# Two engines for the first Q and K copies, masks sooner on VectorE, and two memsets ahead of the first V loads

## The chip, the cores, the metric

One core of a Trainium2 chip. The metric is the device time of one execution in microseconds (us), as a median of runs. A profile's "span" runs from the first to the last instruction of one profiled execution and is some 2 us shorter than the time of that execution.

## The reference

```python
def reference(q, k, v, moe_w_gate, moe_w_val, moe_w_out):   # cut and joined
    scores = q @ k.T / sqrt(64), masked to abs(i - j) <= 32     # 8 batches, 8 heads, 576 x 64
    attn = softmax(scores) @ v
    x = attn with the heads side by side                        # 4608 x 512
    g, val = x @ w_gate, x @ w_val                              # 512 x 1536
    return (g * sigmoid(g) * val) @ w_out                       # 4608 x 512, float32
```

## The kernel before

It works through eight batches: sliding-window attention of a batch, then the feed-forward part on its rows, on TensorE most of the time. The change touches the opening alone: the attention of batch 0, before TensorE has feed-forward work to fill its gaps. Its helpers (cut):

```python
    def cast_qk(st, cast):
        t16 = qk16.tile([128, J9, 2, D], FP16, tag="qk16", name="t16")
        cast(t16.rearrange("p j h d -> p h j d"),
             st.rearrange("p h (j d) -> p h j d", d=D))
        return t16
    def transpose_qk(t16, pool=None):
        ps = (pool or ps_c).tile([128, 2048], FP16, tag="a" if pool is ps_a else "c",
                                 name="qk_ps")
        for j in range(J9):
            nc.tensor.transpose(out=ps[:, 128 * j:128 * j + 128], in_=t16[:, j, :, :],
                                identity=ident)
        return ps[:, 0:J9 * 128].rearrange("c (j a p) -> c a p j", j=J9, a=2)
    def place_k(src, b, half, cast):
        cast(kT[b][:, 2 * half:2 * half + 2, 32:32 + S].rearrange(
            "c a (p j) -> c a p j", j=J9), src)
# place_q: the same into qT, without the offset of 32
# quad_scores(ms, F): 16 score matmuls into a ps_a tile (2 buffers), then two exps on ScalarE
# quad_mask(ms, F): one multiplication by the mask on VectorE
# shift_v(b, m, cast): two copies that build the V tiles which straddle two loads
# pair_av(m): 16 matmuls attention times V, then the normalization on VectorE
# turn_x: transposes of the result, copied to xT by ScalarE
# idle_mms(n): n filler matmuls of 512 columns on TensorE, whose result nobody reads
```

The opening, from the first loads to the first feed-forward unit:

```python
    st = [load_qk2(src, 0, half) for half in range(2) for src in (q, k)]
    nc.gpsimd.memset(v16[1][:, :, :, 64:66], 1.0)
    load_v(0, range(5))
    for s in range(len(SLABS)):
        load_w_slab(moe_w_gate, wg16, s)
        load_w_slab(moe_w_val, wv16, s)
        if s == 1:
            shift_v(0, 0, cast_pool)
    for s in range(4):
        load_wo(s)
    nc.gpsimd.memset(v16[1][0:32, 0, :, :], 0.0)
    nc.gpsimd.memset(v16[1][96:128, NT - 1, :, :], 0.0)
    c16 = [cast_qk(t, cast_dve) for t in st]
    idle_mms(6)
    place_q(transpose_qk(c16[0], ps_a), 0, 0, cast_act)
    idle_mms(2)
    place_k(transpose_qk(c16[1]), 0, 0, cast_act)
    idle_mms(4)
    place_q(transpose_qk(c16[2], ps_a), 0, 1, cast_act)
    quad_scores((0, 1), 0)
    idle_mms(1)
    place_k(transpose_qk(c16[3]), 0, 1, cast_dve)
    quad_scores((2, 3), 0)
    idle_mms(3)
    quad_mask((0, 1), 0)
    quad_scores((0, 1), 1)
    quad_mask((2, 3), 0)
    shift_v(0, 1, cast_dve)
    quad_mask((0, 1), 1)
    idle_mms(2)
    quad_scores((2, 3), 1)
    shift_v(0, 2, cast_act)
    shift_v(0, 3, cast_act)
    quad_mask((2, 3), 1)
    idle_mms(4)
    pair_av(0)
    pair_av(1, ps_a)
    idle_mms(4)
    pair_av(2, ps_a)
    pair_av(3)

    nxt = [qkst.tile([128, 2, J9 * D], FP32, tag="qkst", name="qk_st") for _ in range(4)]
    for t in nxt:
        nc.vector.memset(t[:, 0, 0:1], 0.0)
    st = [load_qk2(src, 1, half, nxt[2 * half + i]) for half in range(2)
          for i, src in enumerate((q, k))]
    for m in range(4):
        turn_x([m], ps_o, cast_act)
    c16 = [cast_qk(t, cast_pool) for t in st]
    load_v(1, range(5))
    for u in range(FKS):
        ffn1_unit(0, u)
        ...
```

The four loads of Q and K bring the first half of Q, the first of K, the second of Q and the second of K; they are called slices here. PSUM is the memory of the tiles that TensorE's matmuls write in these traces (qk_ps, s_ps, o_ps, xt_ps, gv_ps). Loads from SyncE (load_qk2) move float32 as it is. Loads from GpSimd (V, the weights wg, wv, wo) cast to 16 bits on the way, and GpSimd issues them one after the other, in program order. The weights come in five slabs of columns; unit u of the feed-forward part needs slab 0 for u = 0, slab 1 for u = 1 and 2, slab 2 from u = 3, slab 3 from u = 6, slab 4 from u = 9.

Of the kernel before, what the change touches and what calls it, by code (L numbers as in the profile page):

```python
# [132 lines left out]
def kernel(  # L133
# [10 lines left out]
    nc = tc.nc  # L144

    B, H, S, D = q.shape
# [4 lines left out]
    NT = S // 64  # L151
# [5 lines left out]
    J9 = S // 64  # L157
# [13 lines left out]
    ps_a = fast.enter_context(tc.tile_pool(name="ps_a", bufs=2, space=bass.MemoryType.PSUM))  # L171
# [5 lines left out]
    kT = [const.tile([128, HP, S + 64], FP16, name=f"kT{i}") for i in range(2)]  # L177
    qT = [const.tile([128, HP, S], FP16, name=f"qT{i}") for i in range(2)]
    v16 = [const.tile([128, NT, H, 66], FP16, name=f"v16{i}") for i in range(2)]
# [32 lines left out]
    def load_qk2(src, b, half, st=None):  # L212
        if st is None:
            st = qkst.tile([128, 2, J9 * D], FP32, tag="qkst", name="qk_st")
        nc.sync.dma_start(out=st, in_=src[b, 4 * half:4 * half + 4].rearrange(
            "(f h) (p j) d -> (h p) f (j d)", h=2, j=J9))
        return st
# [15 lines left out]
    def load_v(b, ms):  # L233

        src, dst = v[b].rearrange("h s d -> s h d"), v16[b % 2]
        for m in ms:
            if m == 0:
                nc.gpsimd.dma_start(out=dst[32:128, 0, :, 0:D], in_=src[0:96])
            elif m == 4:
                nc.gpsimd.dma_start(out=dst[0:96, 8, :, 0:D], in_=src[480:576])  # L240
            else:
                nc.gpsimd.dma_start(out=dst[:, 2 * m, :, 0:D],
                                    in_=src[128 * m - 32:128 * m + 96])

    def shift_v(b, m, cast):

        vb, t = v16[b % 2], 2 * m + 1
        cast(vb[0:64, t, :, 0:D], vb[64:128, t - 1, :, 0:D])
        cast(vb[64:128, t, :, 0:D], vb[0:64, t + 1, :, 0:D])
# [12 lines left out]
    def load_wo(s):  # L262
        nc.gpsimd.dma_start(
            out=wo16[:, 3 * s:3 * (s + 1), :],
            in_=moe_w_out.rearrange("(f p) c -> p f c", p=128)[:, 3 * s:3 * (s + 1), :])
# [11 lines left out]
# [14 lines that stand above are left out]
    def place_q(src, b, half, cast):  # L291
        cast(qT[b][:, 2 * half:2 * half + 2].rearrange("c a (p j) -> c a p j", j=J9), src)
# [4 lines that stand above are left out]
# [10 lines left out]
    def score_mms(s, c, m, i, g):  # L307

        b, t = divmod(2 * m + i, NT)
        for e in range(2):  # L310
            half = slice(64 * e, 64 * e + 64)
            nc.tensor.matmul(out=s[:, e, c, :],  # L312
                             lhsT=kT[b % 2][half, g, 64 * t:64 * t + 128],
                             rhs=qT[b % 2][half, g, 64 * t:64 * t + 64],
                             start=True, stop=True)

    def exp_act(o, s):
        nc.scalar.activation(out=o, in_=s, func=AF.Exp, bias=0.0, scale=1.0 / float(D) ** 0.5)  # L318
# [19 lines left out]
    def quad_scores(ms, F):  # L338

        if ms not in quads:  # L340
            quads[ms] = ppool.tile([128, 2, 2, 2, HP, 64], FP16, tag="p2", name="p2_t", bufs=2)
            for n, m in enumerate(ms):
                pts[m] = quads[ms][:, n]
        s = ps_a.tile([128, 2, 8, 64], FP32, tag="a", name="s_ps")
        for n, m in enumerate(ms):
            for i in range(2):
                for f in range(2):
                    score_mms(s, 4 * n + 2 * i + f, m, i, 2 * F + f)
        four = slice(128 * F, 128 * F + 128)
        pv = quads[ms].rearrange("p n e i g q -> p e n i (g q)")  # L350
        for e in range(2):
            exp_act(pv[:, e, :, :, four],
                    s[:, e].rearrange("p (n i f) q -> p n i (f q)", n=2, i=2))

    def quad_mask(ms, F):
        four = slice(128 * F, 128 * F + 128)
        pm = quads[ms].rearrange("p n e i g q -> p (n e i) (g q)")[:, :, four]
        nc.vector.tensor_tensor(out=pm, in0=pm, in1=mask.rearrange("p (a f) q -> p a (f q)", f=2),  # L358
                                op=ALU.mult)
# [3 lines left out]
    def pair_av(m, pool=None, normed=True):  # L363
        p = pts.pop(m)
        if pool is ps_o:
            o = [ps_o.tile([128, 264], FP32, tag="o", name="o_ps") for _ in range(2)]
        else:
            t2 = (pool or ps_c).tile([128, 2, 512], FP32, tag="a" if pool is ps_a else "c",
                                     name="o_ps")
            o = [t2[:, 0, 0:264], t2[:, 1, 0:264]]  # L370
        for h in range(H):
            for i in range(2):
                b, t = divmod(2 * m + i, NT)
                nc.tensor.matmul(  # L374
                    out=o[h // 4][64 * i:64 * i + 64, 66 * (h % 4):66 * (h % 4) + 66],
                    lhsT=p[:, place(b, h)[0], i, place(b, h)[1], :],
                    rhs=v16[b % 2][:, t, h, :],
                    start=True, stop=True)
        if pool is ps_o:
            av_ps[m] = [(o[a].rearrange("p (a h e) -> p a h e", a=1, e=66), slice(a, a + 1))  # L380
                        for a in range(2)]
        else:
            av_ps[m] = [(t2[:, :, 0:264].rearrange("p a (h e) -> p a h e", e=66), slice(0, 2))]
        if normed:
            pair_norm(m)
# [291 lines left out]
    def idle_mms(n):  # L677
        ob = ps_o.tile([128, 512], FP32, tag="o", name="warm")
        mf = mask.rearrange("p a q -> p (a q)")
        for _ in range(n):  # L680
            nc.tensor.matmul(out=ob, lhsT=mf[:, 0:128], rhs=mf[:, 0:512], start=True, stop=True)
# [34 lines left out]

    st = [load_qk2(src, 0, half) for half in range(2) for src in (q, k)]
    nc.gpsimd.memset(v16[1][:, :, :, 64:66], 1.0)
    load_v(0, range(5))
    for s in range(len(SLABS)):  # L720
        load_w_slab(moe_w_gate, wg16, s)
# [2 lines left out]
            shift_v(0, 0, cast_pool)  # L724
    for s in range(4):
        load_wo(s)
    nc.gpsimd.memset(v16[1][0:32, 0, :, :], 0.0)
    nc.gpsimd.memset(v16[1][96:128, NT - 1, :, :], 0.0)
    c16 = [cast_qk(t, cast_dve) for t in st]
    idle_mms(6)  # L730
    place_q(transpose_qk(c16[0], ps_a), 0, 0, cast_act)
    idle_mms(2)
    place_k(transpose_qk(c16[1]), 0, 0, cast_act)
    idle_mms(4)
    place_q(transpose_qk(c16[2], ps_a), 0, 1, cast_act)
    quad_scores((0, 1), 0)
    idle_mms(1)
    place_k(transpose_qk(c16[3]), 0, 1, cast_dve)
    quad_scores((2, 3), 0)
    idle_mms(3)  # L740
    quad_mask((0, 1), 0)
    quad_scores((0, 1), 1)
    quad_mask((2, 3), 0)
    shift_v(0, 1, cast_dve)
    quad_mask((0, 1), 1)
    idle_mms(2)
    quad_scores((2, 3), 1)
    shift_v(0, 2, cast_act)
    shift_v(0, 3, cast_act)
    quad_mask((2, 3), 1)  # L750
    idle_mms(4)
    pair_av(0)
    pair_av(1, ps_a)
    idle_mms(4)
    pair_av(2, ps_a)
    pair_av(3)

# [1 line left out]
# [7 lines that stand above are left out]
# [227 lines left out]
```

## Time and profile before

| kernel before | |
|---|---|
| time, first three runs | 320.48 us median, 319.91 to 320.63 |
| span of the profiled execution | 317.8 us, mean granted TensorE clock 0.993 |
| TensorE busy | 303.6 us, 96% |
| first feed-forward matmul (gv_ps, L427) | 21.84 us |
| fourth slice of Q and K landed | 10.6 us |
| wv's slab 3 landed (issued 17.05) | 30.8 us |

A line of a timeline gives start, duration, engine, source line, operation, what it writes and reads, the count, and in brackets how long the engine sat idle before it and what ended that. In the page's strip of 40 slices a digit is tenths; PEclk is the clock granted to TensorE. The other lines of before stand in the prediction. Two more are needed later, the first feed-forward matmul and the strip of the clock:

```profile
21.84 1.02 PE L427 MATMUL gv_ps<-xT,wg 128*128 128x512 f16 x4 [0.69 <-ACT xT L268]
```

```profile
PEclk9999999999999999999999999999999999999997
```

### The profile page before, as it was taken

The page shows a single profiled execution, that of the slowest core. Times are in us where ns is not written, and L with a number is a line of the kernel's source. Part 1 is how long each engine was busy: PE and PEld are TensorE (multiplying, and loading weights), DVE is VectorE, ACT ScalarE, POOL GpSimd, SP SyncE. Part 2 cuts the span into 40 slices and gives each one's busy share as a digit, 9 for nine tenths or more (in the row PEclk, how much of TensorE's full clock was granted, in tenths as well). Part 3 has the DMA queues.
Part 4 walks back from the last instruction along what each step waited for, and adds up shares of the span by engine and source line. Part 5 has one row for each costly group of instructions (what it writes and reads, how often), then busy time and mean ns, then how long its engine had stood idle before and what let it go on. Part 6 is the DMA issues. An engine that isn't in the chain of part 4 may idle for free.

```text
span 317.8 us, 8145 instructions
## 1 busy us (share of the span) xinstructions
PE 303.6 (96%) x3220; PEld 213.2 (67%) x3220; DVE 219.1 (69%) x404; ACT 192.7 (61%) x309; POOL 182.4 (57%) x231
## 2 busy tenths in 40 slices
PE   5779999999999999999999999999999999999991
PEld 3444555676877687768776877677767776777581
DVE  2654398788866787678757885887588958737760
ACT  3774559665756575667466846684668566336530
POOL 8973678649358934994489339953440538303300
PEclk9999999999999999999999999999999999999997
DMA  7999999999959996999799989999651330030012
GB/s 274 166 192 296 244 179 177 200 143 165 158 136 128 172 163 142 121 183 152 164 132 161 159 171 124 136 175 163 153 127 42 95 92 3 24 110 0 0 51 92
DMA packets 155916, 44.22 MB, mean 139 GB/s; under 512 B 136416, under 2 KB 153312, under 8 KB 155872
## 3 DMA queue, kind: packets, MB, share of 16 engines
q0 software_dynamic: 100640, 16.52, 79.3%
q1 hardware_dynamic: 55232, 27.11, 40.7%
q8 instruction: 27, 0.44, 0.6%
q14 instruction: 17, 0.14, 0.2%
HBM read 37.75 MB, written 9.44 MB: 148 GB/s over the span
## 4 chain that ended last, share of the span: by engine, by line
PE 88%; DVE 4%; DMA 3%; ACT 2%; issue 1%; SPq 0%; ACTq 0%
PE gv_ps L553 26%; PE gX_ps L484 13%; PE x_ps L627 12%; PE y_ps L627 9%; PE gZ_ps L484 7%; PE gv_ps L427 6%; PE o_ps L374 4%; PE gY_ps L484 3%; PE ob L441 3%; PE s_ps L312 3%; DMA qk_st<-in_k_dram 3%; PE xt_ps L414 1%; DVE s_top L595 1%; PE z_ps L627 1%; DVE p_t L358 1%
## 5 line engine op out<-in xcount | busy, mean ns | idle before, releaser
L553 PE MATMUL gv_ps<-xT,wv 128*128 128x512 f16 (+1 forms) x224 | 57.2, 349 | 0.0
L553 PE MATMUL gv_ps<-xT,wg 128*128 128x512 f16 x192 | 49.4, 379 | 0.0
L542 POOL TENSOR_TENSOR x_sums<-xT 128x512 f16<-128x512 f16 x14 | 17.4, 1246 | 49.1 <-DVE xT L271 29.3
L595 POOL TENSOR_TENSOR s_top<-hT 128x256 f16<-128x256 f16 x32 | 21.6, 674 | 40.1 <-PE gY_ps L484 28.8
L318 ACT ACTIVATE p_t<-s_ps 128x1024 f16<-128x1024 f32 (+1 forms) x40 | 34.7, 924 | 14.2 <-PE s_ps L312 14.2
L268 ACT ACTIVATE kept<-gX_ps 128x512 f32<-128x512 f32 x48 | 28.6, 595 | 18.1 <-PE gX_ps L484 18.1
L567 DVE TENSOR_TENSOR hT<-ssb,gv_ps 128x512 f16<-128x512 f16 x48 | 32.7, 682 | 9.9 <-ACT ssb L559 9.9
L559 ACT ACTIVATE ssb<-gv_ps 128x512 f16<-128x512 f32 x48 | 28.6, 596 | 17.1 <-PE gv_ps L553 17.1
L506 DVE TENSOR_TENSOR gate<-gX_ps,kept 128x512 f32<-128x512 f32 x24 | 16.6, 692 | 25.9 <-PE gX_ps L484 17.0
L553 PEld LDWEIGHTS <-wv 128*128 128x128 f16 x224 | 21.9, 98 | 17.9
L484 PEld LDWEIGHTS <-g_top 128*128 128x128 f16 x288 | 27.5, 98 | 6.6 <-ACT kept L268 1.5
L627 PEld LDWEIGHTS <-hT 128*128 128x128 f16 x288 | 27.4, 98 | 5.3 <-issue 0.3
L627 PEld LDWEIGHTS <-s_top 128*128 128x128 f16 x288 | 27.7, 98 | 4.1 <-issue 0.6
L511 ACT ACTIVATE silu<-gate 128x512 f16<-128x512 f32 x24 | 15.1, 630 | 24.5 <-DVE gate L506 24.5
L484 PE MATMUL gX_ps<-x_sums,g_top 128*128 128x256 f16 x192 | 28.8, 273 | 0.0
L553 PEld LDWEIGHTS <-wg 128*128 128x128 f16 x192 | 17.6, 98 | 14.6
L501 DVE TENSOR_TENSOR val<-gY_ps,kept 128x512 f16<-128x512 f32 x24 | 16.5, 687 | 14.8 <-ACT kept L268 13.6
L223 POOL DMA_DIRECT2D tok<-in_q_dram x30 | 25.8, 860 | 1.1 <-DMA wo<-in_moe_w_out_dram 1.1
L223 POOL DMA_DIRECT2D tok<-in_k_dram x30 | 25.9, 862 | 0.5 <-DMA wo<-in_moe_w_out_dram 0.5
L392 DVE TENSOR_TENSOR x<-o_ps,rall 128x512 f16<-128x512 f32 x36 | 24.9, 691 | 1.2
L627 PE MATMUL x_ps<-w_top,s_top 128*128 128x256 f16 x192 | 23.6, 273 | 0.0
L322 DVE TENSOR_TENSOR p_t<-p_t,mask 128x1024 f16<-128x1024 f16 x32 | 21.4, 705 | 1.8 <-ACT p_t L318 1.1
(114 smaller groups left out, 618.4 us busy)
## 6 DMA issues: line engine op xcount, KB each, us to landing
out_dram<-osb SPq DMA_DIRECT2D x32, 256.0 KB, 3.1
v<-v SPq DMA_DIRECT2D x12, 264.0 KB, 5.7
v<-in_v_dram POOLq DMA_DIRECT2D x24, 128.0 KB, 7.1
tok<-in_q_dram POOLq DMA_DIRECT2D x24, 128.0 KB, 6.3
tok<-in_k_dram POOLq DMA_DIRECT2D x24, 128.0 KB, 6.5
qk_st<-in_q_dram SPq DMA_DIRECT2D x4, 576.0 KB, 6.9
qk_st<-in_k_dram SPq DMA_DIRECT2D x4, 576.0 KB, 9.1
v<-in_v_dram POOLq DMA_DIRECT2D x16, 96.0 KB, 6.7
```

Of the source, the lines that this page charges most:

```text
L223: nc.gpsimd.dma_start(out=t[0:n].rearrange("p (h d) -> p h d", d=D), in_=src[b].rearrange("h s d -> s h d")[128 * m:128 * m + n])
L268: nc.scalar.activation(out=o, in_=i, func=AF.Copy, bias=0.0, scale=1.0)
L318: nc.scalar.activation(out=o, in_=s, func=AF.Exp, bias=0.0, scale=1.0 / float(D) ** 0.5)
L322: nc.vector.tensor_tensor(out=flat, in0=flat, in1=mask, op=ALU.mult)
L392: nc.vector.tensor_tensor(out=x16s[m][:, a], in0=ov[:, :, :, 0:D], in1=r.unsqueeze(3).to_broadcast([128, a.stop - a.start, 4, D]), op=ALU. ...
L427: nc.tensor.matmul(out=gv[:, i, :], lhsT=w[:, g, 128 * fk:128 * fk + 128], rhs=xts[j][:, g, :], start=(g == 0), stop=(g == GS - 1))
L484: nc.tensor.matmul(out=k[name][:, n], lhsT=lhs[:, g, 128 * n:128 * n + 128], rhs=rhs[:, g, :], start=(first and n == 0 and g == 0), stop=( ...
L553: nc.tensor.matmul(out=k["gv"][:, i, c], lhsT=w[:, g, 128 * fk:128 * fk + 128], rhs=xts[j][:, g, c], start=(g == 0 and c.start == 0), stop ...
L559: nc.scalar.activation(out=k["s"], in_=k["gv"][:, 0, :], func=AF.Silu, bias=0.0, scale=1.0)
L567: "m": lambda: nc.vector.tensor_tensor(out=hts[j][:, fk, :], in0=k["s"], in1=k["gv"][:, 1, :], op=ALU.mult)}
L595: tt = lambda o, a, b, op: (eng or nc.vector).tensor_tensor(out=o, in0=a, in1=b, op=op)
L627: nc.tensor.matmul(out=dst[n], lhsT=lhs[:, f, 128 * n:128 * n + 128], rhs=rhs[:, f, :], start=(first and f == 0 and (split or n == 0)), st ...
```

## The change

Its intent: in the opening, take work off whichever engine holds the chain. The second Q copy goes from ScalarE to VectorE; the second K copy is split between ScalarE and VectorE; the scores that need only the first halves, and their masks, come before the fourth transposes; the V loads start behind two memsets, so that they do not disturb the Q and K loads; and two filler matmuls fewer stand between the groups of attention times V.

```diff
--- before.py
+++ after.py
@@ -716,6 +716,8 @@
 
     st = [load_qk2(src, 0, half) for half in range(2) for src in (q, k)]
     nc.gpsimd.memset(v16[1][:, :, :, 64:66], 1.0)
+    nc.gpsimd.memset(v16[1][0:32, 0, :, :], 0.0)
+    nc.gpsimd.memset(v16[1][96:128, NT - 1, :, :], 0.0)
     load_v(0, range(5))
     for s in range(len(SLABS)):
         load_w_slab(moe_w_gate, wg16, s)
@@ -724,34 +726,35 @@
             shift_v(0, 0, cast_pool)
     for s in range(4):
         load_wo(s)
-    nc.gpsimd.memset(v16[1][0:32, 0, :, :], 0.0)
-    nc.gpsimd.memset(v16[1][96:128, NT - 1, :, :], 0.0)
-    c16 = [cast_qk(t, cast_dve) for t in st]
+    c16 = [cast_qk(t, cast_dve) for t in st[:3]]
     idle_mms(6)
     place_q(transpose_qk(c16[0], ps_a), 0, 0, cast_act)
     idle_mms(2)
     place_k(transpose_qk(c16[1]), 0, 0, cast_act)
     idle_mms(4)
-    place_q(transpose_qk(c16[2], ps_a), 0, 1, cast_act)
+    place_q(transpose_qk(c16[2], ps_a), 0, 1, cast_dve)
+    c16.append(cast_qk(st[3], cast_dve))
     quad_scores((0, 1), 0)
+    idle_mms(3)
+    quad_scores((2, 3), 0)
+    quad_mask((0, 1), 0)
     idle_mms(1)
-    place_k(transpose_qk(c16[3]), 0, 1, cast_dve)
-    quad_scores((2, 3), 0)
-    idle_mms(3)
-    quad_mask((0, 1), 0)
+    src = transpose_qk(c16[3])
+    for a, cast in enumerate((cast_act, cast_dve)):
+        cast(kT[0][:, 2 + a, 32:32 + S].rearrange("c (p j) -> c p j", j=J9), src[:, a])
+    idle_mms(2)
+    quad_mask((2, 3), 0)
     quad_scores((0, 1), 1)
-    quad_mask((2, 3), 0)
+    quad_scores((2, 3), 1)
     shift_v(0, 1, cast_dve)
     quad_mask((0, 1), 1)
-    idle_mms(2)
-    quad_scores((2, 3), 1)
     shift_v(0, 2, cast_act)
     shift_v(0, 3, cast_act)
     quad_mask((2, 3), 1)
     idle_mms(4)
     pair_av(0)
     pair_av(1, ps_a)
-    idle_mms(4)
+    idle_mms(2)
     pair_av(2, ps_a)
     pair_av(3)
```

## The prediction

> **What bounds the kernel now.** I read the page first, then the chain of work that ended last (whole, and for the first 60 us), then the timelines of VectorE, ScalarE, GpSimd and TensorE for the first 42 us, and last the DMA view in short windows.
>
> ```profile
> PE 303.6 (96%) x3220; PEld 213.2 (67%) x3220; DVE 219.1 (69%) x404; ACT 192.7 (61%) x309; POOL 182.4 (57%) x231
> PE 88%; DVE 4%; DMA 3%; ACT 2%; issue 1%; SPq 0%; ACTq 0%
> ```
>
> TensorE sets the time: 96% busy, 88% of the chain. The change touches nothing after the feed-forward part starts (matmuls gv_ps, L427), so all it can win lies ahead of that start, at 21.84 us of a span of 317.8. This is the chain there (start, duration, what):
>
> ```profile
> 2.35 8.24 DMA qk_st<-in_k_dram
> 10.62 0.77 DVE t L271
> ...
> 13.43 1.95 DVE p_t L358 x2
> ...
> 16.05 0.70 DVE p_t L358
> ...
> 16.80 0.58 PE o_ps L374 x24
> 17.38 0.97 PE warm L681 x4
> 18.34 0.82 PE o_ps L374 x32
> 19.16 0.34 PE xt_ps L414 x4
> ...
> 19.53 2.27 ACT xT L268 x4
> 21.79 0.04 issue
> 21.84 8.79 PE gv_ps L427 x40
> ```
>
> It waits for the second half of K until 10.6, then runs on VectorE (cast, copy of K, masks, V copies, a mask) until 16.75, then through attention times V, four filler matmuls, more attention times V, a transpose and four ScalarE copies. VectorE and ScalarE in the same stretch:
>
> ```profile
> 12.15 1.36 DVE L271 COPY kT<-qk_ps 128x1152 f16<-128x1152 f16 x1 [0.77 <-PE qk_ps L287]
> 13.43 1.95 DVE L358 TENSOR_TENSOR p_t<-p_t,mask 128x1024 f16<-128x1024 f16 x2
> 15.41 0.61 DVE L271 COPY v<-v 64x512 f16<-64x512 f16 x2
> ```
>
> ```profile
> 9.43 1.13 ACT L268 ACTIVATE qT<-qk_ps 128x1152 f16<-128x1152 f16 x1 [0.27 <-PE qk_ps L287]
> 10.45 1.08 ACT L318 ACTIVATE p_t<-s_ps 128x512 f16<-128x512 f32 x2
> 12.49 1.09 ACT L318 ACTIVATE p_t<-s_ps 128x512 f16<-128x512 f32 x2 [0.96 <-PE s_ps L312]
> 14.02 2.06 ACT L318 ACTIVATE p_t<-s_ps 128x512 f16<-128x512 f32 x4 [0.43 <-PE s_ps L312]
> 16.11 2.59 ACT L268 ACTIVATE v<-v 64x512 f16<-64x512 f16 x4
> ```
>
> ScalarE's exps end at 16.08, its four V copies at 18.70. The second group of attention matmuls cannot finish without the last of these copies: it ends at 19.16, 0.46 us after it. So ScalarE is a second path, as late as the chain that is shown.
>
> Why K came at 10.6 is in the DMA view. From 4 to 5.5 us the Q and K loads move large packets at 401 GB/s; from 8.6 to 10 the small packets of the V loads have the engines:
>
> ```profile
> DMA packets 279, 0.60 MB, mean 401 GB/s; under 512 B 18, under 2 KB 18, under 8 KB 279
> ```
>
> ```profile
> DMA packets 1631, 0.23 MB, mean 162 GB/s; under 512 B 1621, under 2 KB 1621, under 8 KB 1631
> ```
>
> The third Q/K load (let go at 7.85) and the fourth (10.6) are thus 2.75 us apart, where 0.59 MB at 390 GB/s takes 1.5.
>
> [...] the first V issue takes 1.35 us beside a VectorE cast, later ones 0.76; the first masks, beside two GpSimd V copies (13.21 to 14.83), take 0.94 and 1.09 us, the later ones 0.69. [...]
>
> **The change part by part.** The order of instructions on each engine confirms the moves.
>
> *Second Q copy from ScalarE to VectorE.* ScalarE loses 1.13 us before its exps, so the first pair of exps starts when its scores are done (9.73) and not at 10.45. VectorE gets the copy at 9.41 and is busy to about 10.7 (1.28 to the next instruction, as the K copy had). Only then comes the fourth cast: 10.72 to 11.48, before 10.62 to 11.38. So K's earlier landing buys nothing here: the Q copy ahead of it on VectorE takes its place as the wait.
>
> *Scores (2,3) ahead of the fourth transposes.* They need the score buffer that the Q copy frees at 10.7, so end near 11.2; their exps run 11.25 to 12.3 instead of 12.49 to 13.58.
>
> *K copy over two engines.* Fourth transposes 11.54 to 12.2 (0.68). VectorE does the first mask meanwhile, 11.5 to 12.2, then its half of K to 12.95; ScalarE does its half 12.3 to 12.95. K is whole at 12.95, before at 13.43. The last scores start there, and the four exps end at 12.95 + 0.45 + 2.06 = 15.5, against 16.08: **0.6 us** on ScalarE's path. The V copies then end at 15.5 + 2.59 = 18.1 against 18.70.
>
> *Masks.* The first two are out of the way by 13.6, without a GpSimd copy beside them. Then VectorE needs V chunks one and two.
>
> *Two memsets ahead of the V loads.* 0.53 us each when alone (24.23 and 24.81 now); beside VectorE casts I take 0.2 to 0.5 more in sum, so the V loads begin 1.1 to 1.6 later. V then lands roughly 1.3 later: the third V issue begins near 6.8 and takes 6.2 to land, so 13.0 becomes 14.2. VectorE waits from 13.6 to 14.2, copies V to 14.8, and GpSimd's own V copies (13.21 now, 14.3 then) fall on VectorE's V copies and last masks, at 0.3 to 0.7. So the last two masks end at about 15.5 to 16.2 and 16.2 to 16.9, against 16.75 and 17.34. The memsets at the old place waited on nothing important: GpSimd was idle 3.40 us after them. Weight loads go out 1.3 later too; slab 0 lands near 17.6 instead of 16.3, needed at 21.
>
> *Filler matmuls.* Two fewer between the groups of attention times V: 0.97 falls to 0.48 on that path.
>
> *Sum.* VectorE's path: masks 0.4 to 1.1 earlier and 0.5 less filler, so it is ready 0.9 to 1.6 earlier. ScalarE's: 0.6 earlier. The later one decides: last attention group ends at 18.1 + 0.46 = 18.55, one transpose 0.35, four ScalarE copies 2.27, so the first gv_ps matmul is at 21.25 instead of 21.84. The whole program then ends **0.6 us** earlier.
>
> **The rivals.**
> (a) *Nothing arrives at the end.* The feed-forward start is earlier, but a DMA holds TensorE later: GpSimd's first cast of the next batch's Q ends at 29.90 and TensorE wants it at 30.47, and the last two wo loads let GpSimd go at 43.3 and 45.3 while TensorE needs them at 47.04. The Q load is issued after VectorE's last normalization, which comes earlier too, and the engines are saturated either way, so I give 0.5 us slack a fair chance to survive. If not: 320.3 to 320.6.
> (b) *V becomes the wait.* If V lands over 2 us later, ScalarE's last V copy (needs the fifth V load, near 14.1 now) or the attention matmuls that need GpSimd's copies wait; the gain shrinks to 0 or turns to a loss of up to 0.7: 320.5 to 321.2. Against it: V's packets find the engines free of Q and K by then.
> (c) *The filler matter.* [...] costing one or two us: 321 to 322. [...]
> (d) *More is won.* If GpSimd's copies miss the masks and the scores come as early as the buffers allow, 1 us: 319.4.
>
> **Range and chances.** Base 320.48; its three runs spread over 0.72 us, more than the gain, so the median itself is good to some 0.3. Main case 320.48 - 0.6 = 319.9. I weigh (a) and (b) together at a quarter, (d) at a fifth, (c) at a twentieth. Range 319.0 to 320.8. Two per cent would be 6.4 us, a third of all that comes before the feed-forward part; nothing in the change removes that. Faster 0.01, same 0.985, slower 0.005.
>
> **What would show it.** First gv_ps matmul near 21.25 (right: 20.9 to 21.5). First V issue at 5.5 to 6.1; fourth Q/K load no longer what the fourth cast waits for, and that cast at 10.7 behind the Q copy; exps ending near 15.5; VectorE idle before its V copies; TensorE's 10 us from then on unchanged. I am wrong if the exps end early but the start does not move (then V or the transposes hold it), if a new TensorE gap shows at 29 or 46 us, or if the granted clock falls.

## The result, and the profile after

| | before | after |
|---|---|---|
| time of six runs each, median | 320.28 | 322.65 |
| lowest to highest | 319.91 to 320.63 | 320.95 to 323.34 |
| span of the profiled execution, clock | 317.8, 0.993 | 321.4, 0.982 |
| first feed-forward matmul | 21.84 | 22.84 |
| first silu of the feed-forward part (ssb) | 23.76 | 26.45 |
| first of the two last z_ps copies on ScalarE | 306.74 | 309.59 |

The ratio is 1.0067, interval 1.0041 to 1.0092. A ratio is the mean time of one kernel's runs over that of the other's of the same rounds, so not quite the ratio of the medians. That is the same within 2%, but a clear loss, 2.4 us by the medians, where I had forecast a gain of 0.6; the time lies outside my range.

Where it went in the profiled pair is read off the last three rows: 1.0 us by the first feed-forward matmul, 2.69 us by the first silu, 2.86 us at the end of TensorE's work. Everything is lost in the first 27 us. (The spans differ by 3.6 us; the other 0.8 come after that, in the last copies and stores, which vary by 1 us over all traces, whatever the kernel.)

The chain of work after, in its first 22 us:

```profile
9.89 1.37 DVE qT L271
...
12.83 0.55 ACT kT L268
13.38 0.02 issue
13.40 0.77 DVE kT L271
...
14.64 2.06 ACT p_t L318 x4
...
18.68 0.64 ACT v L268
19.32 0.04 issue
19.36 0.50 PE o_ps L374 x15
```

The two halves of K do not run side by side: VectorE's begins when ScalarE's has ended (12.71 to 13.37, then 13.40 to 14.16). K is whole 0.7 us later than before (13.43), not 0.5 sooner. The last exps, and behind them ScalarE's V copies and the last attention matmuls, follow: the V copies end 0.6 us later than before (19.31 and 18.70). The other 0.4 us of the late start come after them, where the clock is already halved.

The second loss is in TensorE's clock. The strip, the first feed-forward matmuls, and a table by stretches (busy time of each engine, then granted clock, DMA share, GB/s):

```profile
PEclk9978999999999999999999999999999999999996
```

```profile
22.84 1.86 PE L427 MATMUL gv_ps<-xT,wg 128*128 128x512 f16 x4 [0.69 <-ACT xT L268]
24.50 1.91 PE L427 MATMUL gv_ps<-xT,wv 128*128 128x512 f16 x4
26.21 1.10 PE L427 MATMUL gv_ps<-xT,wg 128*128 128x512 f16 x4
```

```profile
19.00:20.00 1.00, 0.64 (x18) 0.57 (x18) 0.96 (x4) 0.31 (x1) 1.00 (x2) 0.77 1.16 155
20.00:21.00 1.00, 0.83 (x8) 0.67 (x7) 0.86 (x6) 0.56 (x2) 1.00 (x3) 0.50 1.31 180
26.00:27.00 1.00, 1.00 (x5) 0.40 (x4) 0.00 (x0) 0.55 (x1) 0.67 (x1) 0.82 1.16 316
```

From 19.54 to 26.36 us, two periods of 3.41, the clock is halved, and two groups of four matmuls take 1.9 us where before all take 1.02. So the dip costs some 2.1 of the 2.69 us: 0.4 ahead of the first feed-forward matmul, and 1.7 from there to the first silu (3.61 us in place of 1.92). In the profile before, the clock drops only in its last slice.

What GpSimd did with the two memsets:

```profile
5.23 1.06 POOL L720 MEMSET v<- 32x528 f16 x1
6.24 1.04 POOL L238 DMA_DIRECT2D v<-in_v_dram  x1
```

The second memset took 1.06 in place of 0.53 us, beside VectorE's first cast, itself 1.17 in place of 0.76. The first V issue moves from 4.42 to 6.24, yet the fifth V load lands at 14.3 as before (14.1): in both traces V's first packets move between 7.8 and 8.4 us, behind most of those of Q and K, and the time from its first issue to landing shrinks from 6.9 to 4.2 us. The weights do move: wv's slab 3 is issued at 18.05 and not 17.05, and lands at 35.4 and not 30.8. In this trace TensorE comes to it late enough not to wait.

### The profile page after: what moved, and what is told of

Its sections match the earlier page's. It is cut to its first block, busy times and chain, and to the rows that moved or that the text cites.

```text
span 321.4 us, 8141 instructions
## 1 busy us (share of the span) xinstructions
PE 306.0 (95%) x3218; PEld 214.1 (67%) x3218; DVE 220.0 (68%) x405; ACT 192.3 (60%) x309; POOL 182.6 (57%) x231
## 4 chain that ended last, share of the span: by engine, by line
PE 88%; DVE 4%; ACT 3%; DMA 2%; issue 0%; SPq 0%; ACTq 0%
PE gv_ps L553 26%; PE gX_ps L484 13%; PE x_ps L627 12%; PE y_ps L627 9%; PE gZ_ps L484 7%; PE gv_ps L427 6%; PE gY_ps L484 3%; PE o_ps L374 3%; PE s_ps L312 3%; PE ob L441 3%; DMA qk_st<-in_q_dram 2%; ACT p_t L318 1%; PE xt_ps L414 1%; DVE s_top L595 1%; PE z_ps L627 1%; ACT v L268 1%
## 5 line engine op out<-in xcount | busy, mean ns | idle before, releaser
L595 POOL TENSOR_TENSOR s_top<-hT 128x256 f16<-128x256 f16 x32 | 21.6, 676 | 40.9 <-PE gY_ps L484 28.7
L484 PE MATMUL gX_ps<-x_sums,g_top 128*128 128x256 f16 x192 | 28.8, 273 | 0.0
L553 PEld LDWEIGHTS <-wg 128*128 128x128 f16 x192 | 17.6, 98 | 14.6
```

Of the source, the lines that this page charges most:

```text
L484: nc.tensor.matmul(out=k[name][:, n], lhsT=lhs[:, g, 128 * n:128 * n + 128], rhs=rhs[:, g, :], start=(first and n == 0 and g == 0), stop=( ...
L553: nc.tensor.matmul(out=k["gv"][:, i, c], lhsT=w[:, g, 128 * fk:128 * fk + 128], rhs=xts[j][:, g, c], start=(g == 0 and c.start == 0), stop ...
L595: tt = lambda o, a, b, op: (eng or nc.vector).tensor_tensor(out=o, in0=a, in1=b, op=op)
```

## The experiments

Three causes were on the table: (1) the halves of K wait for each other, so the start is late; (2) the clock dips; (3) the memsets make the weights late. Their rivals: the dip is a lottery that every kernel plays; V is what is late; the change does no harm but for the dip. Ratios are against runs of the kernel before in the same job; the three jobs ran on three chips. On these the kernel before itself spread more than at first (319.1 to 324.2), by waits that come and go late in the program, such as a score matmul that waits up to 1.4 us for a transposing DMA (kT<-tok, in the trace of the repeat of before). So the ratios have intervals of about 0.4% either way.

**Job one: what is the loss?**

The kernel before, repeated without an edit.

> The kernel before, once more, for the granted clock of each of its runs. All theories: ratio 1.000 within 0.002. If the clock dip at 19.5 to 26.4 us of the changed kernel comes from the change, no run here has one: every clock at or above 0.990, first gv_ps matmul at 21.8 within 0.3 us. If the dip is a lottery that any kernel can draw, some runs here show clocks of 0.98 to 0.985 and 1.5 to 2 us more.

Measured: ratio 0.9965 (0.9931 to 0.9999), first feed-forward matmul at 21.46, clocks 0.993 to 0.998. No dip. What I had not reckoned with: the fourth slice of Q and K landed at 10.2 here, not 10.6. And one kernel against itself comes out 0.35% fast, with an interval that just leaves out 1: a ratio of this size shows nothing by itself.

The changed kernel, repeated without an edit.

> The changed kernel once more. Theory: two costs. A fixed one, about 1.0 us, because the second half of K comes whole 0.7 us later than before (VectorE's half waits for ScalarE's half), so the first gv_ps matmul is again at 22.6 to 23.0; and one that varies, up to 1.7 us, from a stretch of half clock of one or two periods of 3.41 us between 16 and 30 us. Then clocks differ from run to run (0.980 to 0.995) and the ratio is 1.004 to 1.009. Rival, that only the later start costs: every run about 1.0 us longer, ratio 1.003, clocks as before.

Measured: ratio 1.0012 (0.9978 to 1.0047), below what I expected, beside runs of before with a median of 320.81; lowest time 320.81, against 319.52 for the repeat of before. The trace has the halves one after the other again (12.97 to 13.62, 13.66 to 14.42), the first feed-forward matmul at 22.61, and the clock halved for one period, 22.17 to 25.58. Clocks of the seven runs: 0.988 to 0.998. So there is a fixed part, and a dip that comes in some runs.

Four fillers again:

```diff
     pair_av(1, ps_a)
-    idle_mms(2)
+    idle_mms(4)
     pair_av(2, ps_a)
```

> The changed kernel with four filler matmuls again in place of two between the groups of attention times V. If the two missing fillers cause the dip of the clock: clocks of 0.990 and above in all runs, first gv_ps matmul still near 22.8 (ScalarE's V copies set it, not the fillers), 0.8 to 1.2 us over before, ratio 1.0025 to 1.004. Rival, that TensorE's waits for the late K and V copies cause it: the dips stay, ratio 1.005 to 1.009.

Measured: ratio 1.0006 (0.9971 to 1.0041), less than I expected, clocks 0.993 to 0.998 in all six runs, no dip. But the repeat of after, with two fillers, has a sure dip in two of seven runs only (the traced one and the one at 0.988), so this pair does not settle what the fillers do. The start came at 21.91 and not 22.8; half of this is due to the third slice of Q and K, which landed at 7.5 in place of 8.3, and half to the missing dip, not to the fillers on the path: from the third group of transposes to the first feed-forward matmul it is 13.18 us, as in the repeat of after (13.24), whose dip begins later, and 13.67 in after, whose dip lies in that stretch. And 11 us later TensorE lost 0.99 us in a wait that neither profile of the two kernels had shown, for wv's slab 3.

K's halves in two PSUM tiles:

```diff
-    src = transpose_qk(c16[3])
     for a, cast in enumerate((cast_act, cast_dve)):
-        cast(kT[0][:, 2 + a, 32:32 + S].rearrange("c (p j) -> c p j", j=J9), src[:, a])
+        one = (ps_o if a else ps_c).tile([128, 1024 if a else 2048], FP16,
+                                         tag="o" if a else "c", name="qk_ps")
+        r = slice(64 * a, 64 * a + 64)
+        for j in range(J9):
+            nc.tensor.transpose(out=one[:, 64 * j:64 * j + 64],
+                                in_=c16[3][r, j, :, :], identity=ident[r, r])
+        cast(kT[0][:, 2 + a, 32:32 + S].rearrange("c (p j) -> c p j", j=J9),
+             one[:, 0:576].rearrange("c (j p) -> c p j", j=J9))
```

> The changed kernel with the two halves of K's transposes in two PSUM tiles, so that the two copies need not wait for each other (18 transposes of 64 columns in place of 9 of 128). If the wait of VectorE's half for ScalarE's half is what makes the start late: both halves run side by side, the last scores start at 13.4 to 13.6 in place of 14.2, the exps end near 16.0 in place of 16.7, the first gv_ps matmul is at 21.9 to 22.3 in place of 22.84, ratio 1.000 to 1.004. Rival, that V or the Q copy holds the start: it stays at 22.6 or later.

Measured: ratio 1.0033 (0.9995 to 1.0071). The mechanism is right and the sum is not. ScalarE's half and VectorE's, from the timelines of this run:

```profile
12.41 0.66 ACT L268 ACTIVATE kT<-qk_ps 128x576 f16<-128x576 f16 x1
```

```profile
12.29 0.76 DVE L271 COPY kT<-qk_ps 128x576 f16<-128x576 f16 x1
```

They run at the same time, the last scores start at 13.12, and TensorE's timeline says:

```profile
21.29 1.02 PE L427 MATMUL gv_ps<-xT,wg 128*128 128x512 f16 x4 [0.69 <-ACT xT L268]
...
34.89 1.04 PE L427 MATMUL gv_ps<-xT,wv 128*128 128x512 f16 x4 [1.71 <-DMA wv<-in_moe_w_val_dram]
```

The start is at 21.29, within 0.04 us of what I had predicted for the change. From the third transposes it is 12.42 us, 0.76 less than with the halves in line. Then all of it is given back, and more, in one wait of 1.71 us for wv's slab 3, which landed at 34.9.

So the wait between the halves comes from their common PSUM tile. I also built, and did not run, a form in which both still read one tile and VectorE's half writes elsewhere: its wait for ScalarE stayed in the program. The wait is one that the framework put there. The halves lie in alternate 64 columns of one tile on all 128 partitions. What the chip would do without the wait no run here shows; that two tiles do without it, this one does (starts at 12.41 and 12.29, where after has 12.71 and 13.40).

**Job two: the weights.**

K's halves in two tiles, and the memsets back at their old place behind load_wo (a_kpm); the changed kernel with only the memsets back (a_mset); the kernel before with only the memsets moved ahead of load_v (b_mset); the kernel before with only two fillers fewer (b_fill2). The edit of a_mset, b_mset being its reverse:

```diff
     nc.gpsimd.memset(v16[1][:, :, :, 64:66], 1.0)
-    nc.gpsimd.memset(v16[1][0:32, 0, :, :], 0.0)
-    nc.gpsimd.memset(v16[1][96:128, NT - 1, :, :], 0.0)
     load_v(0, range(5))
     ...
     for s in range(4):
         load_wo(s)
+    nc.gpsimd.memset(v16[1][0:32, 0, :, :], 0.0)
+    nc.gpsimd.memset(v16[1][96:128, NT - 1, :, :], 0.0)
```

> The changed kernel with K's halves in two PSUM tiles as in a_kpar, and the two memsets back behind the weight loads. Theory: a_kpar's early start (first gv_ps matmul 21.3) was given back by a 1.7 us wait for wv's fourth slab, which landed at 34.9, since the memsets put the weight loads 1.0 to 1.6 us later. Without them the slab lands by 32, there is no such wait, the first gv_ps matmul is at 21.0 to 21.6, and the ratio is 0.996 to 1.000 (clock dips aside). Rival, that the faster start alone makes it wait for weights: the wait stays at 1 us or more, ratio 1.002 or above.

> The changed kernel with the two memsets back behind the weight loads, K's halves still one after the other. Theory: no wait for wv (slab four by 32), but the start stays late (22.2 to 22.9) and the clock can dip; ratio 1.001 to 1.005. Rival, that the memsets and late V loads make the late start: first gv_ps matmul near 21.8.

> The kernel before with only the two memsets moved ahead of the V loads. Theory: the start hardly moves (21.4 to 22.0), since V lands as early as before (fifth load near 14.2), but wv's fourth slab lands at 34 to 35.5 and TensorE waits 0.5 to 1.7 us for it near 33.5; ratio 1.002 to 1.006. Rival, that the memsets are harmless or help (K's last quarter lands sooner): ratio 0.997 to 1.000, no wait.

> The kernel before with only the two filler matmuls taken from between the groups of attention times V. Theory: start unchanged within 0.2 us (ScalarE's V copies set it), and half clock in the first 30 us in some of the runs[...]; ratio 1.000 to 1.004. Rival, that the fillers lie on the path: start 0.4 us earlier, ratio 0.998 to 0.999, no dip.

Measured:

| run | ratio (interval) | start | wv slab 3 landed | wait for it | clock dip in the trace |
|---|---|---|---|---|---|
| a_kpm | 1.0054 (1.0011 to 1.0097) | 21.80 | 28.8 | none | 21.14 to 24.55 |
| a_mset | 1.0024 (0.9972 to 1.0076) | 22.80 | 26.7 | none | 22.45 to 25.86 |
| b_mset | 1.0059 (1.0005 to 1.0113) | 21.08 | 34.6 | 1.68 us | none |
| b_fill2 | 0.9989 (0.9942 to 1.0035) | 20.98 | 28.3 | none | none |

b_mset settles the memsets: moved alone, in the kernel before, they cost a wait at the same place as in a_kpar. Its start, 21.08, came sooner than I expected (21.4 to 22.0), but b_fill2 starts sooner still and has no such wait, so it is not the early start alone. This is its TensorE:

```profile
34.64 1.04 PE L427 MATMUL gv_ps<-xT,wv 128*128 128x512 f16 x4 [1.68 <-DMA wv<-in_moe_w_val_dram]
```

and with the memsets at the old place no trace has it. My rival for a_mset, that late V makes the late start, falls: its start is as late as after's. a_kpm has neither a late weight nor halves in line, and yet the largest mean loss of the changed forms in the three jobs: five of its six runs have clocks of 0.984 to 0.988, and the sixth, the traced one (0.992), has the dip of the table. My range for it (0.996 to 1.000) had set dips aside, and missed for them. The start missed too (21.80, expected by 21.6), since the third slice came late; from the third transposes it is 12.42 us, as in a_kpar.

b_fill2 missed in one point: I expected an unchanged start. It is at 20.98, but its fourth slice of Q and K landed at 9.25, sooner than in any other trace of the kernel before and its forms, and from the fourth cast to the start it takes 11.71 us, no less than before (11.22). So no gain of the fillers shows. Dips: one or two of its six runs (0.987, and 0.991 perhaps).

**Job three: the sum of causes, a better version, and why the weights come so late.**

a_kpm4 is a_kpm with idle_mms(4). b_kpar is the kernel before with only the K split of a_kpar in place of its place_k; b_kparf adds idle_mms(3) ahead of pair_av(3). a_kq is a_kpar with the next batch's Q and K loads asked for after two feed-forward units. Its edit (the computation is the same, the order is meant to be a bad one):

```diff
-    for t in nxt:
-        nc.vector.memset(t[:, 0, 0:1], 0.0)
-    st = [load_qk2(src, 1, half, nxt[2 * half + i]) ...]
     for m in range(4):
         turn_x([m], ps_o, cast_act)
-    c16 = [cast_qk(t, cast_pool) for t in st]
-    load_v(1, range(5))
     for u in range(FKS):
         ffn1_unit(0, u)
+        if u == 1:
+            (the five lines taken away above)
```

> The changed kernel with all three suspects taken away: K's halves in two PSUM tiles, the memsets back behind the weight loads, four filler matmuls again. Theory of three causes (late start 0.76 us, weights 1.0 to 1.7 us, clock dip up to 1.7 us): no dip (every clock 0.992 or more), no wait for wv, feed-forward start 12.4 us after the third group of transposes, ratio 0.997 to 1.001. Rival, that something else in the change costs: ratio 1.003 or more.

> The kernel before with only K's last copy split over two engines and two PSUM tiles. Theory: VectorE's 1.28 us before its first mask become 0.7, so the first gv_ps matmul comes 0.3 to 0.6 us sooner after the fourth cast (11.2 us there, 10.6 to 10.9 here); ratio 0.997 to 1.000. Rival: ScalarE's half delays its exps and eats the gain (11.2 or more), ratio 1.000 to 1.002.

> As b_kpar, with three more filler matmuls ahead of the last group of attention times V, where TensorE waits for ScalarE's V copies. Theory: same start as b_kpar, and no dip of the clock in any run, so the narrowest spread; ratio 0.996 to 0.999. Rival: the fillers delay that group, start 0.3 to 0.6 us later than b_kpar's.

> a_kpar with the loads of the next batch's Q and K asked for some 5 us later (after two products of the feed-forward part), for the mechanism and not for the time. If wv's fourth slab lands late because these loads share the engines with it: it lands at 28 to 31 in place of 34.9 although it is issued at 17.6 as in a_kpar, and TensorE waits for the next batch's Q later in its place. If it is late because of its issue alone: it lands at 33.5 or later.

Measured: a_kpm4 1.0017 (0.9972 to 1.0061), clocks 0.991 to 0.996 (I had asked for 0.992), no dip in the trace, slab 3 at 30.4 and no wait for it, start 12.41 us after the third transposes. With the three causes taken away the difference from before can no longer be told from none; its median, 321.02, stands beside 321.10. The interval would still allow a loss of 0.6%.

b_kpar 1.0015 (0.9972 to 1.0059): from the fourth cast to the start 11.20 us, where before has 11.22. The rival was right: ScalarE's half sits among its exps and takes what VectorE gains. b_kparf 1.0001 (0.9963 to 1.0040), 11.58 from the fourth cast: the three fillers delay the last group by 0.4 us, as its rival said. No version is shown to beat the kernel before.

One more cost is in the traces, and it was not on my list: the second Q copy. In a_kpm4 the fourth slice landed at 10.2, but VectorE had the Q copy to do first:

```profile
9.99 1.36 DVE L271 COPY qT<-qk_ps 128x1152 f16<-128x1152 f16 x1 [0.80 <-PE qk_ps L287]
11.27 0.75 DVE L271 CAST t<-qk_st 128x1152 f16<-128x1152 f32 x1
```

So the fourth cast came 1.1 us after the landing; over all eight traces of the changed kernel and its forms it is 0.7 to 1.6. Where ScalarE does the Q copy, as in b_mset, the cast starts as the slice lands:

```profile
9.89 0.76 DVE L271 CAST t<-qk_st 128x1152 f16<-128x1152 f32 x1 [1.19 <-DMA qk_st<-in_k_dram]
```

From the fourth cast to the start a_kpm4 takes 10.43 us, where the kernel before takes 11.2. So the change, mended, wins 0.8 us behind the fourth cast and loses about as much ahead of it. No run puts the Q copy back alone: this is read from the traces and not tested.

a_kq took 330.86 us in its one run: TensorE now waits 4.60 us for the next batch's Q, and the clock is halved for three periods (21.08 to 27.91 and 38.15 to 41.56). It is there for one line, wv's slab 3 in the DMA view (size, us from issue to landing), in a_kpar and in a_kq:

```profile
wv<-in_moe_w_val_dram POOLq DMA_DIRECT2D x1, 384.0 KB, 17.3
```

```profile
wv<-in_moe_w_val_dram POOLq DMA_DIRECT2D x1, 384.0 KB, 10.7
```

Issued at 17.59 and 17.79, it lands at 34.9 and 28.5. So the slab is late because the next batch's Q and K loads, asked for at about 20 us, share the engines with what is left of the weights by then. (The next batch's V loads moved with them, but a_kpar issues those from 36.87 us on, after the slab has landed.) With the memsets in front, slab 3 is issued 0.6 to 1.3 us later and lands 3 to 8 us later (pairs of one job). From issue to landing, the median of three such wv slabs of 384 KB was 10.5 us in a_mset, 13.7 in before and 17.3 in after. An explanation that fits is that a later issue leaves more of the weights for the crowded time; the 6.4 us between a_kpar and a_kq, one trace each, agree with it, and no run tests it by itself.

**How often the clock dips.** Traces without a dip have mean clocks of 0.993 to 0.997; in before the 0.993 is all half clock at the program's end (its last 4.3 us), and I take the difference among the others to be of that kind, which was not checked. A mean of 0.990 or less is therefore taken as a dip. That count is on the low side: two of the traces with a dip have 0.991 and 0.992, values near what the end alone would give (0.992 in after, from half clock over its last 4.9 us). Of the 37 runs of the six kernels with two fillers between the groups (after, a_again, a_kpar, a_mset, a_kpm, b_fill2), 12 have it; of the 70 runs of the kernels with four (b_again, before in three jobs, a_fill4, b_mset, a_kpm4, b_kpar, b_kparf), 3. With 0.992 as the limit it is 20 of 37 and 11 of 70. The rate is not the same in all of the first (a_kpar none of six, a_kpm five), so the fillers are not alone in it. The one pair that differs in the fillers alone and dipped often, a_kpm against a_kpm4, has five of six against none of six (with 0.992: six against two), but the two ran in different jobs on different chips. So the fillers' part in the dip is likely and not shown. From the clock records the periods of 3.41 us can be laid over each trace, counted from where the clock rises to full (5.88 to 8.80 us); the first dip of each trace that has one starts four periods later. I counted the columns of matmuls that ended in each, a matmul on half the array for half: the first dips followed periods with 2,576 (a_again), 3,038 (a_kpm), 2,543 (a_mset), 2,608 (after) and 3,104 (a_kq) columns, with TensorE busy for 1.74 to 2.08 of the 3.41 us, where a period full of feed-forward matmuls has 8,192 (26.36 to 29.77 in after: sixteen of 512), and no trace dipped after one with 3,200 or more. Two traces did not dip after 2,560 (b_fill2) and 3,055 (a_kpm4), so a thin period came before each first dip and did not always bring one; some matmul records can be missing from a trace.

If a thin period has a part in the dip, which these runs do not settle, it would explain why the start and the fillers act together. Between the last filler and the first feed-forward matmul TensorE has only narrow matmuls and transposes. That stretch is 18.35 to 21.84 before, 3.5 us, and 17.93 to 22.84 after, 4.9 us. A period of 3.41 us almost never falls wholly into the first, and often into the second. By these two lengths alone, if the periods lie at random, an estimate is 3% and 44% of runs. It is a sketch: in after itself the thin period (16.12 to 19.53) began before the stretch and held its two fillers.

## Why the prediction was wrong, by its own steps

- *TensorE bounds, only the opening can change*: held. The stretch from the first silu to the first of the two last z_ps copies, nearly all TensorE's, took 282.98 us before and 283.14 after.
- *The second Q copy goes to VectorE and holds the fourth cast*: held. The copy took 1.36 us, the fourth cast followed it at 11.16 (I had 10.72; the third slice of Q and K landed 0.45 later in that execution). What it costs was mis-sized: 0.1 us against the one late landing that I had (10.62), 0.7 to 1.6 us after the landing in the eight traces with the copy on VectorE.
- *"K is whole at 12.95"*: **failed**, and it is the first step that did. I added two halves in parallel where the program has them in line. It was knowable without the chip: the listing of the order of instructions with their waits has VectorE's half waiting for ScalarE, and I read the order and not the waits. The lengths of the halves, some 0.65 us on ScalarE and 0.75 on VectorE, were my estimate, and they held (0.66 and 0.76 after). The halves in line cost 0.76 us against halves side by side (13.18 in a_fill4 and 12.42 in a_kpar, from the third transposes to the start). K was whole at 14.16 in the trace after: 0.76 of the 1.21 us are this wait, the rest is the third slice.
- *"The first two masks are out of the way by 13.6", the last two by 16.2 and 16.9*: **failed** with K. They ended at 14.76, 16.77 and 17.43, the last two no sooner than before (16.74 and 17.34).
- *V lands 1.3 us later*: **failed**, without harm: 14.3 against 14.1. V's packets moved behind those of Q and K in both traces, so its issue had slack.
- *"Weight loads go out 1.3 later too; slab 0 lands near 17.6 ... needed at 21"*: **failed** by what it left out. The delay of the issue was right (11.22 for 9.89; slab 0's wv landed at 16.7, sooner than I had it), but I checked the first slab and not the one with least slack. Slab 3 had 2.8 us of it (landed 30.8, used from 33.56), and a delay of 1 us at the issue became 4.6 at the landing. In the profiled pair this cost nothing, the dip having made TensorE late; in runs without a dip it is up to 1.0 us (a_fill4), and 1.7 if the start is early. Rival (a), a DMA that holds TensorE later, was right in kind, and named other DMAs (the next Q, the last wo loads).
- *Rival (c), one in twenty, that the fillers matter, "costing one or two us"*: the clock did fall, and I had held it unlikely by the wrong test. I looked for a long gap without any work; that such a gap is what it takes was an assumption of mine that no trace had shown. In the trace after, the period before the dip has none longer than 0.82 us, and TensorE is busy for 2.0 of its 3.41. The dip cost 2.1 us in the profiled pair (0.4 before the first feed-forward matmul, 1.7 after it), and comes in some runs only. The two fillers whose loss I counted as 0.5 us off the path were probably part of what kept the period full, which is not shown; on the path they were not, since ScalarE's V copies came later.
- *A reading of the trace*: "later ones 0.76" fits the issues of the weights. The V issues after the first took 0.78 to 1.41 us.
- *The base*: of four traces of the kernel before and its two edited forms (the one I was given, b_again, b_mset, b_fill2), mine had the latest fourth slice of Q and K (10.6; the others 10.2, 9.9 and 9.25). The start follows it by 11.2 us (11.7 in b_fill2). So the opening of before is often better than the one trace said, and part of the 0.6 us that I saw to be won comes by itself when that slice lands sooner. Even without the three faults the change shows no gain (a_kpm4).

What stays open: how much of the mean loss each cause has over many runs, since they overlap (a dip hides the wait for the weights) and the late waits for DMA in all kernels are as large; what decides whether the clock dips, and the fillers' part in it; and what the second Q copy costs by itself.

## What to carry to other kernels

Work that is split over two engines is parallel only if the program has no wait between the parts: look at the waits of the built program, not only at its order, and give each part its own PSUM tile (here that took 0.76 us off the start). When an issue on a queue moves, follow every later transfer on that queue to its use, and look first at the one with the least slack; a small delay can grow where a second stream is about to join (here 1 us became 4.6). Filler matmuls that look like cost on the path may be what holds the clock: look at the thinnest whole period of TensorE as well as at the longest gap (12 of 37 runs dipped with two fillers and 3 of 70 with four, so that the fillers did hold it is likely here, not shown), and look at several traces before trusting a start that depends on a DMA.
